# Cosformer attention and a gated feed-forward layer on one core: the q tails through GpSimd's queue, one q load moved behind the x transposes, the last product in two column pieces

## The chip, the core and the metric

The kernel runs on one core of a Trainium2 chip. A core has five engines that take their instructions in order, each from its own queue: TensorE (PE; its weight loads are shown apart as PEld), VectorE (DVE), ScalarE (ACT), GpSimd (POOL) and SyncE (SP). They wait for one another by semaphores. Sixteen DMA engines move data between HBM and the core's SBUF; DMAs are issued from the queues of SP, ACT and GpSimd. The metric is the device time of one execution in microseconds, the median of the runs.

## The reference

q, k and v are (8 batches, 8 heads, 576 positions, 64) in float32. The output is (4608, 512), one row for each batch and position.

```python
def phi(x, c, s):
    r = np.maximum(x, 0.0)
    return np.concatenate([r * c, r * s], axis=-1)
q_p, k_p = phi(q, cos_w, sin_w), phi(k, cos_w, sin_w)
kv = np.einsum('bhsf,bhsd->bhfd', k_p, v)
z = np.sum(k_p, axis=2)
num = np.einsum('bhsf,bhfd->bhsd', q_p, kv)
den = np.einsum('bhsf,bhf->bhs', q_p, z)[..., None] + 1e-06
x = (num / den).transpose(0, 2, 1, 3).reshape(B * S, H * D)

rms = np.sqrt(np.mean(x * x, axis=-1, keepdims=True) + 1e-06)
xn = x / rms * rms_g
g = xn @ w_gate
silu = g * (1.0 / (1.0 + np.exp(-g)))
out = (silu * (xn @ w_val)) @ w_out
```

w_gate and w_val are (512, 1536), w_out is (1536, 512).

## The kernel before

**Blocks.** The 4608 rows are worked through in nine blocks of 512 rows, in the order 0, 1, 2, 3, 4, 5, 6, 8, 7. Block b below 8 holds the first 512 positions of batch b. The last 64 positions of all eight batches, the tails, are 8 x 64 = 512 rows, and they are block 8. (Of batch 0 the tail is every ninth position.)

**A block** has 12 steps (`gval_step`) and an output part (`out_step`). In step n, PE forms the n-th 128 columns of the gate product and of the value product (`half_mm`, L565), four matmuls of 512 columns each, in two pairs of PSUM banks (`psG`, `psV`) by turns; ScalarE takes the silu of one (L579) and VectorE multiplies it with the other into `hT` (L580). `out_step` forms the product with w_out as seven smaller products (`prod`, L664) of sums of `hT` with sums of w_out; `side`, `q_start`, `q_end` and, in block 7, `last_part` add their results up in `osb`, and `store` writes them to HBM.

**The attention of later batches** lies in the slots of the earlier blocks. The order is written out by hand: `at(block, step, place, function, ...)` enters a call, and `run` issues it when the block gets there. Steps 12 to 17 are places in `out_step`; "post" of step 14 comes behind "post" of step 13. For batch nb from 3 on:

- Load k, v and q into `raw` (`load_kv`, `load_q`, on SP's queue) in block nb - 2, at steps 4, 6 and 8, but in block 1 (batch 3) at steps 4, 5 and 7 (lines 940 to 946).
- The feature maps of k (`k_phi`, L300 on ScalarE and L302 on VectorE) and the cast of v (`v_cast`) run from the output part of block nb - 2 into steps 0 and 1 of block nb - 1.
- In steps 0 to 3 of block nb - 1 the feature maps of q (`q_phi`, to `qp`) and their DMA transposes on SP's queue (`q_tr_dma`, L354, to `qpT`); in step 3 k times v (`kvz_pe`, L396).
- In steps 4 to 10 of block nb - 1 the four products of q with it (`nd_pe`, L458), each followed by the division (`nd_post`, L498 to L508), the sum of squares on ScalarE (`x_sq`, L524), its power -0.5 on GpSimd (L529), the norm on VectorE (`x_norm`, L536) and the DMA transpose of the rows on SP's queue (`x_tr_dma`, L549), the last of them at step 12. Block nb takes them as `xnT`; its first matmul needs all four. (For batch 2 the steps differ by one or two; the products of batch 7 are in block 8.)

**The tails of q** are loaded in four pairs of batches, each pair by two DMAs of 128 KB in rows of 256 bytes (`load_q_tails`, L147, on SP's queue), at steps (5, 9), (6, 1), (6, 2) and (6, 4). In block 6 follow their feature maps (`q_tails_phi`, steps 3, 4, 5, 7), their DMA transposes into the buffer of the k features (`q_tails_tr_dma`, L364, printed as `kp<-qp`), and at steps 5, 7, 9 and 11 the products (`nd_tails_pe`, L483).

**The ring.** k, v, q and each pair of tails take a buffer `raw` from a ring of four; a load waits until what stood in the buffer four loads earlier has been read.

**The end.** In block 7 the last products go to separate banks. `q2[1]` is a copy of the first product of the second half of the rows; products 6 and 7 are added to the copy and to the original, and `last_part` (L1015) subtracts and stores each of the four quarters of 256 columns.

Of the kernel before, what the change touches and what calls it, by code (L numbers as in the profile page):

```python
# [9 lines left out]
FP32 = mybir.dt.float32  # L10
BF16 = mybir.dt.bfloat16
AF = mybir.ActivationFunctionType
ALU = mybir.AluOpType
# [4 lines left out]
def kernel(  # L18
# [11 lines left out]
    nc = tc.nc  # L30
    B, H, S, D = q.shape
    DM = H * D
    DFF = moe_w_gate.shape[1]
    P = 128
# [3 lines left out]
    NC5 = 5  # L38
# [8 lines left out]
    V, A, G = nc.vector, nc.scalar, nc.gpsimd  # L47
# [3 lines left out]
    ring = ctx.enter_context(tc.tile_pool(name="ring", bufs=4))  # L51
# [7 lines left out]
    psG = [ps.tile([P, 512], FP32, name=f"psG{i}") for i in range(2)]  # L59
    psV = [ps.tile([P, 512], FP32, name=f"psV{i}") for i in range(2)]  # L60
    psC = [ps.tile([P, 512], FP32, name=f"psC{i}") for i in range(2)]
# [29 lines left out]
    raw = {}  # L91

    def raw_tile(which, b):
        if (which, b) not in raw:
            t = ring.tile([P, H * NC5 * D], FP32, name="raw", tag="raw")
            raw[(which, b)] = t
        return raw[(which, b)]
# [40 lines left out]
    rqt = {}  # L138

    def load_q_tails(pair):  # L140
        t = ring.tile([P, H * NC5 * D], FP32, name="raw", tag="raw")
        rqt[pair] = t[:, 0 : H * D].rearrange("p (h d) -> p h d", h=H)
        for i in range(2):
            src = q[2 * pair + i, :, 512:576, :].rearrange("h s d -> s h d")
            if 2 * pair + i == 0:
                src = q[0].rearrange("h (s c) d -> s h c d", c=NC)[:, :, NC - 1, :]
            nc.sync.dma_start(out=rqt[pair][64 * i : 64 * i + 64, :, :], in_=src)  # L147

    g4 = one.tile([4, P], FP32, name="g4")
    nc.scalar.dma_start(out=g4[:, :], in_=moe_rms_g.rearrange("(t p) -> t p", p=P))  # L150
    for c0, c1 in ((0, 4), (4, NC)):
        nc.sync.dma_start(
            out=raw_kv("k", 0)[:, :, c0 * D : c1 * D],
            in_=kv_rows(k, 0, (0, HP))[:, :, c0 * D : c1 * D],
# [58 lines left out]
    HC = DM // 2  # L213
# [22 lines left out]
    def g_spread(bank, t):  # L236
# [12 lines left out]
        out=th[:, 0:NTAB], in0=fidx[:, :], scalar1=S - 1.0, scalar2=ang,  # L249
# [341 lines left out]
    def store(blk, j, cols, src, eng=nc.sync):  # L591
        if 0 < blk < 8:
            rows = out[blk * S : blk * S + 512, :].rearrange("(p j) m -> p j m", j=4)
            eng.dma_start(out=rows[:, j, cols[0] : cols[1]], in_=src)
            return
        for i in range(2):
            b, c = (0, 2 * j + i) if blk == 0 else (2 * j + i, NC - 1)
            rows = out[b * S + 512 : b * S + S, :]
            if b == 0:
                rows = out[0:S, :].rearrange("(s c) m -> s c m", c=NC)[:, c, :]  # L600
            eng.dma_start(out=rows[:, cols[0] : cols[1]], in_=src[64 * i : 64 * i + 64])
# [49 lines left out]
    def prod(i, p, dst, first=False, cols=(0, HC)):  # L651
        c0, c1 = p * P, p * P + HC
        lhs = {
            1: (s0, 0, c0), 2: (s12, 0, c1), 3: (hT, 0, c0), 4: (hT, NM, c1),
            5: (s12, 0, c0), 6: (s3, 0, c0), 7: (s4, 0, c0),
        }[i]
        rhs = {2: (0, 0), 5: (NM, HC)}.get(i)
        for m in range(NM):
            t, o, c = lhs
            if rhs:  # L660
                w = wo[:, rhs[0] + m, rhs[1] + cols[0] : rhs[1] + cols[1]]
            else:
                w = wsum[:, {1: 0, 3: 1, 4: 2, 6: 3, 7: 4}[i], m, cols[0] : cols[1]]
            nc.tensor.matmul(  # L664
                dst, lhsT=t[:, o + m, c : c + P], rhs=w,
                start=(first and m == 0), stop=(m == NM - 1), skip_group_check=True,
            )
# [158 lines left out]
    def at(blk, n, where, f, *args):  # L826
        slots.setdefault((blk, n), {}).setdefault(where, []).append((f, args))
# [9 lines left out]
    for j in range(4):  # L837
        at(0, (8, 8, 9, 10)[j], "post", q_phi, V, 1, j, 0)
        at(0, (8, 9, 10, 10)[j], "post", q_phi, A, 1, j, 1)
        bank = (psC[0], psC[1], psV[0], psV[1])[j]  # L840
# [85 lines left out]
            at(b, m, "post", x_tr_dma, nb, j)  # L926

    for pair in range(4):
        at(*((5, 9), (6, 1), (6, 2), (6, 4))[pair], "post", load_q_tails, pair)
        n = (3, 4, 5, 7)[pair]  # L930
        at(6, n, "post", q_tails_phi, V, pair, 0)
        at(6, n, "post", q_tails_phi, A, pair, 1)
        at(6, n, "post", q_tails_tr_dma, pair)
        n = 5 + 2 * pair
        at(6, n, "pe", nd_tails_pe, pair)
        at(6, n, "pre", nd_post, 2 * pair + 1, 4)
        at(6, n, "post", x_sq, 2 * pair + 1, 4)
        at(6, n + 1, "post", x_norm, 2 * pair + 1, 4)
        at(6, n + 1, "post", x_tr_dma, 2 * pair + 1, 4)
    for nb in range(3, B):  # L940
        b = nb - 2
        for which, n in (zip("kvq", (4, 5, 7) if b == 1 else (4, 6, 8))):
            if which == "q":
                at(b, n, "post", load_q, nb)
            else:
                at(b, n, "post", load_kv, which, nb)
# [32 lines left out]
    def out_step(blk):  # L979
        bq = ((psG[0], psV[0]), (psC[0], psC[1]))  # L980
        osb = {}
        mid = slice(HC, 3 * HC)

        def begin(p):
            bank = bq[p][0]
            prod(3, p, bank[:, 0:HC], first=True)
            prod(4, p, bank[:, HC:DM])
            osb[p] = osb_tile()
            A.copy(out=osb[p][:, mid], in_=bank[:, :])
            run(blk, 12 + p, "act")  # L990

        def q_start(p):
            V.tensor_tensor(
                out=bq[p][1][:, 0:HC], in0=osb[p][:, HC : 2 * HC],
                in1=osb[p][:, 2 * HC : 3 * HC], op=ALU.add,
            )

        def side(p):
            A.copy(out=osb[p][:, mid], in_=bq[p][0][:, :])
            if blk == last_blk:  # L1000
                store(blk, p, (HC, DM), osb[p][:, HC : 2 * HC])
                store(blk, p + 2, (0, HC), osb[p][:, 2 * HC : 3 * HC])

        def q_end(p):
            V.tensor_tensor(
                out=osb_ends(p),
                in0=bq[p][1][:, :].rearrange("p (i m) -> p i m", i=2),
                in1=osb[p][:, mid].rearrange("p (i m) -> p i m", i=2), op=ALU.subtract,
            )
            store(blk, p, (0, DM), osb[p][:, 0:DM])  # L1010
            store(blk, p + 2, (0, DM), osb[p][:, DM : 2 * DM])

        def last_part(p, i, bank):
            c = 3 * HC * i
            V.tensor_tensor(  # L1015
                out=osb[p][:, c : c + HC], in0=bank[:, 0:HC],
                in1=osb[p][:, HC * (1 + i) : HC * (2 + i)], op=ALU.subtract,
            )
            store(
                blk, p + 2 * i, (HC * i, HC * i + HC), osb[p][:, c : c + HC],  # L1020
                nc.sync if p == i else nc.scalar,
            )

        def osb_ends(p):
            t = osb[p][:, 0:HC]
            ap = list(t.ap)
            return bass.AP(t.tensor, t.offset, [ap[0], [3 * HC, 2], ap[-1]])

        h_sum12(0, NM // 2)
        h_sum12(NM // 2, NM)  # L1030
        begin(0)
        run(blk, 12, "post")
        begin(1)
        q_start(0)
        h_sum0()
        run(blk, 13, "post")
        prod(5, 0, bq[0][0][:, 0:HC])
        prod(2, 0, bq[0][0][:, HC:DM])
        run(blk, 14, "act")
        side(0)  # L1040
        q_start(1)
        h_sum4()
        prod(5, 1, bq[1][0][:, 0:HC])
        prod(1, 0, bq[0][1][:, 0:HC])
        run(blk, 15, "act")
        last = blk == last_blk
        q2 = (
            (psG[1][:, 0:HC], psV[1][:, 0:HC]) if last
            else (bq[0][1][:, HC:DM], bq[1][1][:, HC:DM])
        )  # L1050
        A.copy(out=q2[0], in_=bq[0][1][:, 0:HC])
        h_sum3()
        run(blk, 14, "post")
        prod(2, 1, bq[1][0][:, HC:DM])
        if last:
            prod(7, 0, bq[0][1][:, 0:HC])
            prod(1, 1, bq[1][1][:, 0:HC])
            A.copy(out=q2[1], in_=bq[1][1][:, 0:HC])
            side(1)
            prod(6, 0, q2[0])  # L1060
            last_part(0, 0, bq[0][1])
            prod(7, 1, bq[1][1][:, 0:HC])
            last_part(0, 1, psG[1])
            prod(6, 1, q2[1])
            last_part(1, 0, bq[1][1])
            last_part(1, 1, psV[1])
            return
        prod(1, 1, bq[1][1][:, 0:HC])
        run(blk, 16, "act")
        side(1)  # L1070
        A.copy(out=q2[1], in_=bq[1][1][:, 0:HC])
        run(blk, 17, "act")
        run(blk, 12, "dve")
        prod(7, 0, bq[0][1][:, 0:HC])
        prod(6, 0, q2[0])
        q_end(0)
        prod(7, 1, bq[1][1][:, 0:HC])
        prod(6, 1, q2[1])
        q_end(1)
        run(blk, 15, "post")  # L1080
# [46 lines left out]
```

## Time and profile before

| What | us |
| --- | --- |
| median of 3 runs | 327.35 (326.6 to 328.78) |
| the profiled execution | 327.93 |
| its span in the trace | 326.2 |

| Engine | busy us | share of the span |
| --- | --- | --- |
| PE | 308.4 | 95% |
| VectorE | 234.1 | 72% |
| ScalarE | 180.3 | 55% |
| GpSimd | 41.4 | 13% |

Positions in the trace are microseconds from the span's start. The value products' first matmul groups of blocks 3, 4 and 5 begin at 122.55, 154.86 and 187.18, so a block takes 32.3 us; the one of block 6 begins at 220.75, and block 6 takes 41.1 us to that of block 8 (261.81). PE is busy for 0.9 or more of most slices of the span; the clock granted to it is full but for one stretch near 235 us and the last 1.5 us.

A line of a view of waits has the engine and line that waited, what it waited for, and us in total, times and longest. A line of the timeline has the start, the length, engine, line, operation, what is written from what, how many instructions were merged, and in brackets the idle time before and what ended it. "SPq" and "POOLq" are instructions that issue DMAs. A line of the windows has the stretch, then busy us of PE, PEld, DVE, ACT and POOL with counts, the granted clock, the DMA share and GB/s.

### The profile page before, as it was taken

How to read it: one execution, taken by the hardware profiler on the slowest of the kernel's cores; microseconds unless marked ns; L12 is line 12 of the kernel's file. 1: busy time of each engine (PE TensorE's matmuls, PEld its weight loads, DVE VectorE, ACT ScalarE, POOL GpSimd, SP SyncE). 2: the span in 40 equal slices, each digit the busy share in tenths (PEclk: the TensorE clock that was granted, in tenths of full speed). 3: DMA queues.
4: the chain of work that ended last, by engine and by line, in shares of the span. 5: the costliest groups of instructions: out<-in, count | busy, mean ns of one | idle time of the engine just before them, and what ended most of it. 6: DMA issues, size and time to landing. Idle time of an engine off the chain costs nothing.

```text
span 326.2 us, 6671 instructions
## 1 busy us (share of the span) xinstructions
PE 308.4 (95%) x2541; PEld 188.1 (58%) x2574; DVE 234.1 (72%) x459; ACT 180.3 (55%) x353; POOL 41.4 (13%) x79
## 2 busy tenths in 40 slices
PE   7899999999799999999999999989299999999995
PEld 2689564546654585458545754665145844574474
DVE  7976977989857786778678867885367747864373
ACT  5766756736764586458655865576245335433331
POOL 9670220002001100110011001100001101100000
PEclk9999999999999999999999999999789999999999
DMA  7999999789969977997779678995933130115003
GB/s 231 237 274 277 269 341 169 218 185 248 176 154 195 191 163 205 200 196 159 198 184 193 186 184 173 192 242 148 188 78 65 18 129 20 32 33 114 0 2 129
DMA packets 80383, 53.80 MB, mean 165 GB/s; under 512 B 52139, under 2 KB 74719, under 8 KB 80351
## 3 DMA queue, kind: packets, MB, share of 16 engines
q1 hardware_dynamic: 73110, 40.99, 59.6%
q0 software_dynamic: 6944, 12.13, 15.3%
q8 instruction: 20, 0.33, 0.5%
q10 hardware_dynamic: 296, 0.26, 0.2%
q14 instruction: 13, 0.10, 0.1%
HBM read 37.83 MB, written 9.44 MB: 145 GB/s over the span
## 4 chain that ended last, share of the span: by engine, by line
PE 77%; DMA 8%; DVE 5%; ACT 4%; issue 3%; SPq 1%; POOL 1%; ACTq 0%; DVEq 0%; POOLq 0%
PE psV L565 23%; PE psG L565 22%; PE psC L664 9%; PE psG L664 6%; PE psV L664 4%; DMA raw<-in_q_dram 3%; DMA hsum<-in_v_dram 2%; PE psV L716 2%; PE psG L716 2%; DVE xn L536 2%; PE psA L458 2%; DMA xnT<-xn 2%; PE psC L583 2%; PE psG L583 2%; PE psA L396 2%
## 5 line engine op out<-in xcount | busy, mean ns | idle before, releaser
L580 DVE TENSOR_TENSOR hT<-psV,sg 128x512 bf16<-128x512 f32 x99 | 68.1, 688 | 56.5 <-PE psV L565 38.0
L579 ACT ACTIVATE sg<-psG 128x512 f32<-128x512 f32 x99 | 58.6, 592 | 76.2 <-PE psG L565 74.7
L565 PE MATMUL psG<-xnT,wg 128*128 128x512 bf16 x330 | 89.1, 382 | 3.7 <-DMA xnT<-xn 1.6
L565 PE MATMUL psV<-xnT,wv 128*128 128x512 bf16 x347 | 90.7, 382 | 0.6 <-issue 0.2
L565 PEld LDWEIGHTS <-wv 128*128 128x128 bf16 x400 | 39.2, 98 | 47.4 <-issue 1.1
L565 PEld LDWEIGHTS <-wg 128*128 128x128 bf16 x400 | 36.7, 98 | 41.3 <-issue 2.9
L664 PEld LDWEIGHTS <-hsum 128*128 128x128 bf16 x480 | 46.0, 98 | 8.0 <-DVE hsum L636 2.1
L529 POOL TENSOR_TENSOR rs<-ms,mhalf 128x1 f32<-128x1 f32 x36 | 21.0, 584 | 226.4 <-ACT scr L524 226.2
L524 ACT ACTIVATE scr<-xt 128x513 bf16<-128x513 f32 x36 | 22.9, 635 | 28.4 <-DVE xt L508 27.5
L300 ACT ACTIVATE kp<-raw,tab 128x256 bf16<-128x256 f32 (+2 forms) x56 | 32.4, 617 | 2.5 <-DMA raw<-in_k_dram 2.5
L536 DVE SCALAR_TENSOR_TENSOR xn<-xt,rs,gb 128x512 bf16<-128x512 f32 (+1 forms) x37 | 26.9, 729 | 1.8 <-POOL rs L529 1.7
L300 ACT ACTIVATE qp<-raw,tab 128x512 bf16<-128x512 f32 (+1 forms) x40 | 26.0, 670 | 1.3 <-DMA raw<-in_q_dram 1.3
L508 DVE TENSOR_TENSOR xt<-psA,rec 128x512 f32<-128x512 f32 x36 | 24.9, 691 | 1.2
L664 PEld LDWEIGHTS <-hT 128*128 128x128 bf16 x192 | 18.4, 98 | 4.7 <-DVE hT L580 0.6
L664 PE MATMUL psV<-wsum,hsum 128*128 128x256 bf16 x144 | 18.7, 273 | 0.1
L302 DVE TENSOR_SCALAR kp<-raw,tab 128x256 bf16<-128x256 f32 (+1 forms) x48 | 17.8, 421 | 0.8 <-DMA raw<-in_k_dram 0.7
L664 PE MATMUL psC<-wsum,hsum 128*128 128x256 bf16 x138 | 17.7, 272 | 0.0
L302 DVE TENSOR_SCALAR qp<-raw,tab 128x512 bf16<-128x512 f32 (+1 forms) x38 | 17.2, 466 | 0.0
L458 PEld LDWEIGHTS <-qpT 128*128 128x128 bf16 x224 | 10.6, 97 | 7.0 <-issue 0.6
L630 DVE TENSOR_TENSOR hsum<-hT 128x1536 bf16<-128x1536 bf16 x16 | 14.5, 949 | 0.0
L664 PE MATMUL psC<-wo,hsum 128*128 128x256 bf16 x96 | 13.1, 273 | 0.0
L565 PE MATMUL psV<-kp,wv 128*128 128x512 bf16 x47 | 12.3, 379 | 0.1
(131 smaller groups left out, 327.0 us busy)
## 6 DMA issues: line engine op xcount, KB each, us to landing
raw<-in_q_dram SPq DMA_DIRECT2D x6, 1024.0 KB, 10.6
out_dram<-osb SPq DMA_DIRECT2D x24, 256.0 KB, 2.7
raw<-in_k_dram SPq DMA_DIRECT2D x5, 1120.0 KB, 7.8
raw<-in_v_dram SPq DMA_DIRECT2D x5, 1120.0 KB, 10.5
out_dram<-osb SPq DMA_DIRECT2D x22, 128.0 KB, 2.4
raw<-in_k_dram POOLq DMA_DIRECT2D x2, 1152.0 KB, 19.0
raw<-in_v_dram POOLq DMA_DIRECT2D x2, 1152.0 KB, 15.4
wg<-in_moe_w_gate_dram POOLq DMA_DIRECT2D x3, 512.0 KB, 14.0
```

What stands on the lines that cost most here:

```text
L300: A.activation(out=out_ap, in_=in_ap, func=AF.Relu, scale=scale)
L302: eng.tensor_scalar(out=out_ap, in0=in_ap, scalar1=scale, scalar2=0.0, op0=ALU.mult, op1=ALU.max)
L458: nc.tensor.matmul(heads[:, g, hp, :], lhsT=qpT[:, h, j * P : (j + 1) * P], rhs=kvzs[b][:, g, hp * E : (hp + 1) * E], start=True, stop=True,)
L508: V.tensor_tensor(out=xt[:, 0:DM].rearrange("p (hp g d) -> p g hp d", g=2, d=D), in0=heads[:, :, :, 0:D], in1=rec[:, :, :].unsqueeze(3).to ...
L524: A.activation(out=scr[:, :], in_=xt[:, 0 : DM + 1], func=AF.Square, scale=1.0 / math.sqrt(DM), accum_out=ms[:, :],)
L529: G.tensor_tensor(out=rs[:, :], in0=ms[:, :], in1=mhalf[:, :], op=ALU.pow)
L536: V.scalar_tensor_tensor(out=xn_of[(b, j)][:, c], in0=x_of[(b, j)][:, c], scalar=rs_of[(b, j)][:, :], in1=gb[:, c], op0=ALU.mult, op1=ALU. ...
L565: nc.tensor.matmul(bank[:, cols[0] : cols[1]], lhsT=w[:, t, n * P : (n + 1) * P], rhs=x[:, t, cols[0] : cols[1]], start=(t == 0), stop=(t ...
L579: A.activation(out=sg[:, :], in_=g[:, 0:TB], func=AF.Silu)
L580: V.tensor_tensor(out=hT[:, n, :], in0=v[:, 0:TB], in1=sg[:, :], op=ALU.mult)
L630: V.tensor_tensor(out=s12[:, m0:m1, :], in0=hT[:, m0:m1, :], in1=hT[:, NM + m0 : NM + m1, :], op=ALU.add,)
L664: nc.tensor.matmul(dst, lhsT=t[:, o + m, c : c + P], rhs=w, start=(first and m == 0), stop=(m == NM - 1), skip_group_check=True,)
```

## The change

There are three edits.

1. The four pairs of q tails go to one `raw` buffer, side by side, in place of four buffers; they are issued from GpSimd's queue, not SP's, and at steps (4, 9), (4, 11), (5, 1) and (5, 3).
2. In block 1 the load of v of batch 3 moves from step 5 to step 8 and that of q from step 7 to step 14, which stands behind the last x transpose of the block in SP's queue.
3. In block 7 the copy of the second half's first product is made in two pieces, of 160 and 96 columns, into two banks, behind `side(1)` and not ahead of it. Product 6 is made for each piece, and `last_part` subtracts and stores each. The queue of a store is given with the call.

```diff
     def load_q_tails(pair):
-        t = ring.tile([P, H * NC5 * D], FP32, name="raw", tag="raw")
-        rqt[pair] = t[:, 0 : H * D].rearrange("p (h d) -> p h d", h=H)
+        t = raw_tile("t", 0)[:, pair * H * D : (pair + 1) * H * D]
+        rqt[pair] = t.rearrange("p (h d) -> p h d", h=H)
...
-            nc.sync.dma_start(out=rqt[pair][64 * i : 64 * i + 64, :, :], in_=src)
+            nc.gpsimd.dma_start(out=rqt[pair][64 * i : 64 * i + 64, :, :], in_=src)
...
-        at(*((5, 9), (6, 1), (6, 2), (6, 4))[pair], "post", load_q_tails, pair)
+        at(*((4, 9), (4, 11), (5, 1), (5, 3))[pair], "post", load_q_tails, pair)
...
-        for which, n in (zip("kvq", (4, 5, 7) if b == 1 else (4, 6, 8))):
+        for which, n in (zip("kvq", (4, 8, 14) if b == 1 else (4, 6, 8))):
...
-        def last_part(p, i, bank):
-            c = 3 * HC * i
+        def last_part(p, i, bank, eng, c0=0, c1=HC):
+            o, t = 3 * HC * i, HC * (1 + i)
             V.tensor_tensor(
-                out=osb[p][:, c : c + HC], in0=bank[:, 0:HC],
-                in1=osb[p][:, HC * (1 + i) : HC * (2 + i)], op=ALU.subtract,
-            )
-            store(
-                blk, p + 2 * i, (HC * i, HC * i + HC), osb[p][:, c : c + HC],
-                nc.sync if p == i else nc.scalar,
-            )
+                out=osb[p][:, o + c0 : o + c1], in0=bank[:, 0 : c1 - c0],
+                in1=osb[p][:, t + c0 : t + c1], op=ALU.subtract,
+            )
+            store(blk, p + 2 * i, (HC * i + c0, HC * i + c1), osb[p][:, o + c0 : o + c1], eng)
...
-            (psG[1][:, 0:HC], psV[1][:, 0:HC]) if last
+            (psG[1][:, 0:HC], None) if last
...
-            A.copy(out=q2[1], in_=bq[1][1][:, 0:HC])
             side(1)
+            cuts = ((psV[1], 0, 160), (psC[0], 160, HC))
+            for bank, c0, c1 in cuts:
+                A.copy(out=bank[:, 0 : c1 - c0], in_=bq[1][1][:, c0:c1])
             prod(6, 0, q2[0])
-            last_part(0, 0, bq[0][1])
+            last_part(0, 0, bq[0][1], nc.sync)
             prod(7, 1, bq[1][1][:, 0:HC])
-            last_part(0, 1, psG[1])
-            prod(6, 1, q2[1])
-            last_part(1, 0, bq[1][1])
-            last_part(1, 1, psV[1])
+            last_part(0, 1, psG[1], nc.scalar)
+            for bank, c0, c1 in cuts:
+                prod(6, 1, bank[:, 0 : c1 - c0], cols=(c0, c1))
+            last_part(1, 0, bq[1][1], nc.sync)
+            last_part(1, 1, *cuts[0][:1], nc.scalar, *cuts[0][1:])
+            last_part(1, 1, *cuts[1][:1], nc.sync, *cuts[1][1:])
```

## The prediction

> **What bounds the kernel now.** I read the page first: TensorE (PE) is busy 95% of the span and its two products of the gate and value weights (L565) lead the chain of waits, so a saving has to be a stretch in which PE stands still. The query of waits, taken for the stretch from 212 to 240 us, names the largest one (columns: engine, line, what it waited for; us in total, times, longest):
>
> ```profile
> ACT sg L579 <- PE psG L565: 10.7, 5, 6.9
> PEld L483 <- DMA kp<-qp: 6.2, 1, 6.2
> PE psA L483 <- DMA kp<-qp: 5.7, 1, 5.7
> ...
> PE psG L565 <- DMA raw<-in_q_dram: 1.1, 1, 1.1
> ```
>
> PE waits 5.7 us in block 6 for the first DMA transpose of the q tails, and 1.1 us before it, where block 6 begins. The timeline of SP's queue shows what stands ahead of both (start us, us, line, operation, count):
>
> ```profile
> 207.21 4.24 SPq L549 DMA_TRANSPOSE xnT<-xn  x1
> 211.50 1.40 SPq L147 DMA_DIRECT2D raw<-in_q_dram  x2
> 212.99 2.36 SPq L549 DMA_TRANSPOSE xnT<-xn  x1
> ...
> 226.37 1.30 SPq L147 DMA_DIRECT2D raw<-in_q_dram  x2
> 227.83 1.26 SPq L354 DMA_TRANSPOSE qpT<-qp  x1
> 229.14 1.34 SPq L147 DMA_DIRECT2D raw<-in_q_dram  x2
> 230.64 1.24 SPq L354 DMA_TRANSPOSE qpT<-qp  x1
> 232.04 2.68 SPq L364 DMA_TRANSPOSE kp<-qp  x2
> ```
>
> From 226.37 on SP issues back to back, and two pairs of tail loads (L147) stand between the transposes. The chain of waits carries the landings (start, us, what), first at the end of block 1, then in blocks 5 and 6:
>
> ```profile
> 83.66 5.42 DMA xnT<-xn
> ```
> ```profile
> 212.28 6.95 DMA raw<-in_q_dram
> ...
> 232.04 3.41 DMA kp<-qp
> 235.45 0.04 issue
> ```
>
> The long wait also costs clock. In windows of 0.5 us the column before the last two is the granted clock; it falls at 232.6, 2.8 us after PE stopped (229.76), and is back at 239.4, 3.9 us after PE went on (235.50):
>
> ```profile
> 232.00:232.50 0.50, 0.00 (x0) 0.00 (x0) 0.00 (x0) 0.00 (x0) 0.00 (x0) 1.00 1.07 219
> 232.50:233.00 0.50, 0.00 (x0) 0.00 (x0) 0.00 (x0) 0.00 (x0) 0.00 (x0) 0.60 1.23 198
> ```
>
> Eight matmuls then took 1.82 + 1.65 us in place of 2 x 0.86: 1.7 us, and with the shorter matmuls about 1.9.
>
> **Block 6, the tails' wait.** Times are counted from the block's first matmul, S (219.73). PE reaches the tails' product at S + 10.0 (229.76). The eight tail loads leave SP's queue. Then the last q transpose goes out as in block 5, where it went out at 195.79 with S = 186.15: S + 9.64, as VectorE ends its half of that q feature map only at S + 9.5 (229.22). It takes 1.24 us to issue. The tails' feature maps end at S + 9.9 on VectorE (229.61), so the first tail transpose is issued at S + 10.95 and lands 3.3 us later (3.41 here with loads beside it, 3.2 the median of q transposes): S + 14.25. PE still waits 4.2 us, not 5.7. Removed: **1.5 us**, the two pairs of loads (1.30 + 1.34 us) less 1.1 that is now spent waiting for VectorE. The next thing that is late is the transpose itself. 4.2 is above the 2.8 us after which the clock fell, so I keep the clock's loss; if it stayed up, 1.9 more would go. If the loads were already in and nothing else were late, the whole 5.7 would go; the S + 9.5 of VectorE excludes that. The ends are 1.0 and 3.4.
>
> **Block 6, its start.** The first pair of tails was issued and moved ahead of the last x transpose (issued 212.99). Without it that transpose goes out at about 212.5 (block 4's 180.30 plus a block period of 32.3) and not behind 256 KB, lands before 218.6, and the 1.1 us go: **-1.1** (ends -1.2 and 0).
>
> **Blocks 4 and 5, the tails through GpSimd.** GpSimd's queue holds little, and its timeline says when it is free:
>
> ```profile
> 172.99 0.55 POOL L529 TENSOR_TENSOR rs<-ms,mhalf 128x1 f32<-128x1 f32 x1 [3.19 <-ACT scr L524]
> 176.73 0.55 POOL L529 TENSOR_TENSOR rs<-ms,mhalf 128x1 f32<-128x1 f32 x1 [3.20 <-ACT scr L524]
> 197.58 0.55 POOL L529 TENSOR_TENSOR rs<-ms,mhalf 128x1 f32<-128x1 f32 x1 [20.30 <-ACT scr L524]
> ```
>
> A DMA issue takes it 0.73 to 1.07 us (the startup's loads). Pair 0 fits between the first two powers (1.5 to 2.1 us of 3.2). The other three pairs come after 177.28 and before 197.58 in its order, and nothing makes them wait: the one buffer was last read in step 3 of block 4 (q of batch 5). So all six issues run at once, from 177.3 to 182 or 184, although two pairs are written into block 5. The powers are not delayed. In the ring of four buffers k, v and q of batch 7 now follow those of batch 6, last read by 196, and are loaded from 198 to 207: no wait.
>
> The transfers are the price. 1 MB in rows of 256 B moved at about 200 GB/s when it was alone (197 to 201 in the windows from 231 to 235): 5.2 us of all 16 engines. From 174.6 to 183.3 these are busy with k, v, q of batch 6 and the x transposes of block 5 (DMA share about 1.1 or more in windows of 1 us, but 0.39 from 178 to 179). The last x transpose was issued at 180.30 and PE needed it at 186.15; its like in block 1 landed 5.42 after its issue, so the slack is near 0.5. Below, the cost is 0, if the tails find gaps; above, it is 5.2 - 0.5 = 4.7 plus 1.9 of clock, as PE would be idle over 2.8 us. I take about half the transfer, 2.5 us, as delay: two queues share the engines, 0.9 us of pair 0 lies in front of the q load, and the gap at 178 takes some. Less the slack: **+2.0**. Nearest row: in block 5 one pair (256 KB, about 1.3 us) ahead of the same transpose, with its issues, made the 1.1 us.
>
> **Block 1, q of batch 3.** k is issued at 68.05 as before; v goes from step 5 to step 8, behind the first x transpose (74.42 to 75.6), and q behind all four. v has 7.8 us (k's landing) and lands at 83.5; ScalarE casts it from 84.54. The last x transpose was ready at 83.37 and issued at 83.66. Its 5.42 us ran while the engines moved 50 GB/s or less from 83.5 to 84.5, so they are mostly its own time, not q's: of PE's 1.57 us I take back 0.3, from the shorter issue of the one ahead. The load of q is now issued near 84.7. A q load on quiet engines (51.46, moved by about 57.7) needs some 6.5 us: it lands at 91.2. ScalarE wants it at 90.5 (90.77 - 0.3), VectorE at 91.9. ScalarE's next silu and what VectorE makes of it wait 0.7 us behind it; VectorE was idle or waiting for PE (0.25 us) before its next product, and its cast ended 0.36 us before PE used it: hidden, nearly. **-0.3** (ends -1.57, and +3.6 below).
>
> **The end.** PE's last product is cut into 160 and 96 columns: 12 matmuls for 6, the same columns, weights loading beside them, **0**. ScalarE copies its start in two pieces (0.14 us fixed from 0.36 and 0.58 for 256 and 512 columns, so 0.28 + 0.22 for 0.36) inside 0.45 us that PE spends on another product: up to +0.1. Its 512-column copy moves ahead, from 320.49 to near 318.9, so two of SP's stores leave 1.6 us earlier. The DMA engines now move six last stores in one burst from 321.9 to 324.3; with these two gone from it, the last 48 KB, issued at 322.5 as VectorE ends (322.61 before), are through by 323.6. **-0.6** (ends -1.0, +0.2).
>
> The sum: -0.3 + 2.0 - 1.1 - 1.5 - 0.6 = **-1.5**. The profiled execution took 327.93 (span 326.2 and 1.7 around it) and would take 326.4; it lies 0.6 above the median of the runs, 327.35, so I predict 325.9.
>
> **The rivals.** *The tails are hidden.* The 2.0 is 0: the transfers fill gaps and the x transpose keeps its 5.4 us. For it: the gap at 178 and the quiet stretch after 183.3; against: the issues end by 184 and the engines are full from 179 to 183. -3.5: 323.9. Chance 0.27.
>
> *The tails block the next block.* The x transposes of block 5 end behind the whole 1 MB: 4.7 us at 186.15, plus 1.9 of clock, from a wait of 2.8 us on. -3.5 + 6.6 = +3.1: 330.5. For it: small rows, all issued in 7 us; against: the two queues are separate and the load of q was there first. Chance 0.14.
>
> *q of batch 3 comes late.* A q load under load landed after 10.6 us: 95.3 here, 4.8 after ScalarE wants it, less some 0.9 of cover, so PE loses 3.9 at the first product with k and v of block 2. -1.5 + 3.9 = +2.4: 329.8. It needs stores or transposes to hold the engines from 85 to 90, where they moved little but x transposes until 87.7. Chance 0.11.
>
> *GpSimd is slow to issue.* If each of the six issues waited out one VectorE sum (0.95 us), the last would go at 186, half of the tails would come behind the x transposes, and the 2.0 would be 0.7: 324.6. Against it, the startup's issues took 0.73 to 1.07 us while VectorE was busy 0.9 to 1.0 of its time. Chance 0.05. The Trainium skill, SBUF — State Buffer, section "🔬 SBUF: two separate sides", warns of such a thing: GpSimd writes the descriptors of its DMAs itself and is locked out while VectorE runs in a two-port mode; by that rule this rival would hold, and the startup's rows do not bear it out.
>
> **How the numbers follow.** The forecast has 0.43, with 324.5 to 327.5 as its own range. Within 1% means 324.1 to 330.6, about what a measurement can tell from no change. Faster than that: most of the first rival (0.20) and the low tail of the forecast (0.07). Slower: half of the second (0.07) and a little of the third (0.03). The range of 8 in 10 runs from 323.5, leaving out a tenth below, to 329.9, leaving out most of the second rival.
>
> **What would show it.** Right: no tail load on SP; PE's wait at L483 about 4.2 us with the clock still falling; block 6 starting without a wait; a new wait of PE for an x transpose at the start of block 5, near 186; GpSimd's eight issues between 173 and 184. Wrong: a wait at L483 under 2.8 us (my order on SP and VectorE fails), block 5 starting on time or over 3 us late, ScalarE waiting over 2 us for q at 90.

## The result and the profile after

The changed kernel takes **331.91 us**, the kernel before on the same chip 327.18 us (median of 4 runs): ratio **1.0127** with an interval of 1.0084 to 1.0170. It is slower by about 4.2 us. The first execution that was profiled ran at half pace (652.62 us) and is not read. The profile below is of a repetition of the same kernel, with a median of 332.22 us beside 328.25 us, ratio 1.0111 [1.0079, 1.0143], and a profiled execution of 332.06 us.

The page (span; busy time and share by engine; granted clock in 40 slices):

```profile
span 330.2 us, 6728 instructions
PE 313.1 (95%) x2580; PEld 188.9 (57%) x2580; DVE 234.3 (71%) x460; ACT 180.3 (55%) x354; POOL 46.5 (14%) x87
PEclk9999999999999999999999969999979999999999
```

The span grew by 4.0 us (326.2 before). The clock has two dips in place of one (near 235 us before, now the second): the new one is in slice 24, from 190 to 198 us, at the start of block 5. PE's own timeline shows what is there, and a smaller stop in block 2 (start, length, engine, line, what; in brackets the idle time before and what ended it):

```profile
93.88 1.08 PE L396 MATMUL psA<-vv,kp 116*128 116x65 bf16 x30 [1.06 <-DVE vv L296]
...
191.55 1.86 PE L565 MATMUL psG<-xnT,wg 128*128 128x512 bf16 x4 [6.07 <-DMA xnT<-xn]
```

PE stops for 6.07 us in front of block 5 and then runs at a lower clock: its first group of four matmuls takes 1.86 us, 1.03 at full clock. The wait in block 6 that the change was aimed at is shorter, not gone (6.2 and 5.7 before):

```profile
PEld L483 <- DMA kp<-qp: 4.9, 1, 4.9
...
PE psA L483 <- DMA kp<-qp: 4.4, 1, 4.4
```

The chain of waits has the landings (start, us):

```profile
85.22 6.25 DMA raw<-in_q_dram
...
179.45 11.97 DMA xnT<-xn
...
237.19 3.40 DMA kp<-qp
```

The last x transpose for block 5 is issued at 179.45, earlier than before (180.30), and takes 11.97 us to land. GpSimd's timeline puts the tail loads (L147) beside it:

```profile
172.84 1.41 POOL L147 DMA_DIRECT2D raw<-in_q_dram  x2
...
176.42 4.09 POOL L147 DMA_DIRECT2D raw<-in_q_dram  x6
```

The starts of the blocks (first gate matmul) give the balance by stage, in us:

| Stretch | before | after | difference |
| --- | --- | --- | --- |
| start to block 1 | 54.54 | 54.21 | -0.33 |
| block 1 | 34.68 | 32.95 | -1.73 |
| block 2 | 32.30 | 33.53 | +1.23 |
| block 3 | 32.31 | 32.31 | 0 |
| block 4, to the start of block 5 | 32.32 | 38.55 | **+6.23** |
| block 5 | 33.58 | 34.61 | +1.03 |
| block 6 | 41.05 | 39.49 | -1.56 |
| block 8 | 31.32 | 31.06 | -0.26 |
| block 7 and the end | 34.05 | 33.49 | -0.56 |

The savings that the change was aimed at are there in small sums. One stretch outweighs them all.

### The profile page after: what moved, and what is told of

It is laid out like the page before. It is cut to its first block, busy times and chain, and to the rows that moved or that the text cites. A ratio compares the mean times of both kernels' runs of the same rounds, so it can differ in the third digit from the quotient of the medians.

```text
span 650.8 us, 6695 instructions
## 1 busy us (share of the span) xinstructions
PE 635.4 (98%) x2547; PEld 296.9 (46%) x2580; DVE 238.6 (37%) x460; ACT 182.1 (28%) x354; POOL 45.0 (7%) x87
## 3 DMA queue, kind: packets, MB, share of 16 engines
q1 hardware_dynamic: 69030, 39.99, 25.0%
## 4 chain that ended last, share of the span: by engine, by line
PE 97%; issue 1%; DMA 0%; DVE 0%; ACT 0%; ACTq 0%
PE psV L565 28%; PE psG L565 28%; PE psC L664 12%; PE psG L664 7%; PE psV L664 5%; PE psV L716 2%; PE psA L458 2%; PE psG L716 2%; PE psA L396 2%; PE psG L583 2%; PE psC L583 2%; PE psC L671 1%; PE psV L372 1%; PE psA L403 1%; DMA kp<-qp 0%
## 5 line engine op out<-in xcount | busy, mean ns | idle before, releaser
L565 PE MATMUL psV<-xnT,wv 128*128 128x512 bf16 x347 | 181.6, 679 | 2.8 <-issue 2.8
L565 PE MATMUL psG<-xnT,wg 128*128 128x512 bf16 x330 | 175.2, 677 | 4.7 <-issue 4.7
L565 PEld LDWEIGHTS <-wv 128*128 128x128 bf16 x400 | 59.2, 148 | 125.9 <-issue 125.9
L565 PEld LDWEIGHTS <-wg 128*128 128x128 bf16 x400 | 55.8, 145 | 101.0 <-issue 99.7
L664 PEld LDWEIGHTS <-hsum 128*128 128x128 bf16 x486 | 71.8, 149 | 40.8
L664 PE MATMUL psC<-wsum,hsum 128*128 128x256 bf16 (+1 forms) x144 | 36.5, 447 | 0.0
L664 PE MATMUL psV<-wsum,hsum 128*128 128x256 bf16 (+1 forms) x144 | 36.4, 448 | 0.0
L664 PE MATMUL psC<-wo,hsum 128*128 128x256 bf16 x96 | 25.8, 433 | 0.0
L565 PE MATMUL psG<-kp,wg 128*128 128x512 bf16 x46 | 24.1, 674 | 0.3 <-issue 0.3
L664 PE MATMUL psG<-wo,hsum 128*128 128x256 bf16 x96 | 24.3, 452 | 0.0
```

The costliest lines, as they stand in the source:

```text
L565: nc.tensor.matmul(bank[:, cols[0] : cols[1]], lhsT=w[:, t, n * P : (n + 1) * P], rhs=x[:, t, cols[0] : cols[1]], start=(t == 0), stop=(t ...
L664: nc.tensor.matmul(dst, lhsT=t[:, o + m, c : c + P], rhs=w, start=(first and m == 0), stop=(m == NM - 1), skip_group_check=True,)
```

## Experiments

Theory: all eight tail loads get ahead of, or in among, the last x transpose of block 5, and PE waits for it. Rivals: q of batch 3 costs the time; the end does; GpSimd's queue itself (its small rows, or its slow issue) is at fault, and not the amount of data in front of the transpose.

**The whole change again** is the profile shown above.

> The changed kernel as it is, for a profile of an ordinary execution and a closer ratio. By the theory that the tails' transfers hold the x transposes of block 5 (T1), PE waits 4 to 5 us for xnT at the start of block 5 and its clock falls there. By the theory that q of batch 3 comes late (T2), PE loses about 4 us in steps 0 to 3 of block 2, with ScalarE waiting 2 to 5 us for raw from q. By the theory that GpSimd's issues hold VectorE or its own powers (T3), the issues of the tails take well over 1 us each and VectorE's instructions beside them are longer than their like in block 3. Ratio about 1.013 by all.

Measured: 1.0111, the wait at block 5 as above, longer than the 4 to 5 us expected.

**The three edits, one by one.** The diffs are the three parts of the change, each alone on the kernel before.

> Only the first edit: tails in one buffer, by GpSimd's queue, at the earlier steps. T1 and T3: the loss is here, ratio 1.015 to 1.02 (+5 to +6 us), as the other edits take 0.3 and 0.6 us off. T2: this edit alone is faster, ratio 0.99 to 0.998 (the prediction's -0.6 to -3 us).

> Only the second edit: v of batch 3 at step 8, q at step 14. T1 and T3: ratio 0.995 to 1.001. T2: ratio 1.010 to 1.018, with the whole loss in block 2.

> Only the third edit: the last product in two column pieces. All theories: ratio 0.997 to 1.000 (the prediction's -0.6 us, ends -1.0 and +0.2). If it is over 1.003, the third edit has a part in the loss that no theory has.

| Edits | median us | ratio |
| --- | --- | --- |
| 1, tails through GpSimd | 333.5 | 1.0162 [1.0133, 1.0190] |
| 2, q of batch 3 | 327.22 | 0.9972 [0.9945, 1.0000] |
| 3, last product in pieces | 327.33 | 0.9987 [0.9961, 1.0013] |

Edit 1 alone makes the kernel slower, by 5.3 us, and has the same wait (6.06 us in front of block 5). The three differences from 1 add up to +0.0121, beside the 1.0127 of the whole: the edits don't act on each other in a way that can be measured. The end alone can't be told from no change in the times; in its profile the last stretch, from the start of block 7, takes 33.5 us (34.05 before).

**The same loads from SP's queue.** Edit 1, but issued from SP's queue, all eight ahead of the last x transpose.

```diff
-            nc.gpsimd.dma_start(out=rqt[pair]..., in_=src)
+            nc.sync.dma_start(out=rqt[pair]..., in_=src)
-        at(*((4, 9), (4, 11), (5, 1), (5, 3))[pair], "post", load_q_tails, pair)
+        at(*((4, 9), (4, 9), (4, 11), (4, 11))[pair], "post", load_q_tails, pair)
```

> The first edit alone, but on SP's queue, with all four pairs in block 4 (steps 9, 9, 11, 11), so that the same 1 MB in rows of 256 bytes is issued ahead of the last x transpose on the same queue. If it is the transfers in front of that transpose that cost (T1, whatever the queue), PE waits 4.5 to 6.5 us at the start of block 5, the clock falls, and the ratio is 1.010 to 1.018 as with GpSimd's queue. If it is something of GpSimd's queue (two queues taking turns on the engines, or GpSimd writing descriptors), the wait is under 4 us and the ratio under 1.008.

Measured: 331.35 us, 1.0106 [1.0066, 1.0146]. SP's queue (start, us, line, count):

```profile
175.49 3.68 SPq L549 DMA_TRANSPOSE xnT<-xn  x1
179.21 8.25 SPq L147 DMA_DIRECT2D raw<-in_q_dram  x8
187.56 1.38 SPq L549 DMA_TRANSPOSE xnT<-xn  x1
```

and PE's timeline:

```profile
191.55 0.59 PE L565 MATMUL psG<-xnT,wg 128*128 128x512 bf16 x1 [4.56 <-DMA xnT<-xn]
```

Here one queue carries both. The transpose stands behind the whole megabyte, is not issued before 187.56, and lands 3.86 us later (chain of waits):

```profile
187.56 3.86 DMA xnT<-xn
```

The kernel to compare with is edit 1 alone, on GpSimd's queue (PE's timeline):

```profile
192.02 1.86 PE L565 MATMUL psG<-xnT,wg 128*128 128x512 bf16 x4 [6.06 <-DMA xnT<-xn]
```

Positions in the two traces can't be set side by side, as block 4 began at 153.48 there and at 154.50 here. From there to the start of block 5 it is 38.5 us with GpSimd's queue, 37.05 with SP's and 32.3 in the kernel before. So data ahead of the transpose is enough for most of the wait without GpSimd's queue; the other 1.5 us come with that queue.

The 3.86 us are not the transpose's time with nothing in front of it: between its issue and 189.75 the engines still moved 0.39 MB, of which the transpose itself has 0.13. In the two versions below that spread the loads out on SP's queue, an x transpose of block 1 landed in 3.5 and 3.4 us. I take 3.86 us as the most that it needs.

**The same bytes in long rows.** Edit 1, with GpSimd's loads in rows of 2 KB in place of 256 bytes, taken from other positions of q. The tails hold other values of q here.

```diff
-            src = q[2 * pair + i, :, 512:576, :].rearrange("h s d -> s h d")
+            src = q[2 * pair + i, 0, 0:512, :].rearrange("(s r) d -> s (r d)", r=8)
```

> The first edit alone, with the same number of bytes a load, but taken from other positions of q in rows of 2 KB and not 256 bytes (so the tails hold other values of q). If the number of small rows sets the cost, the 1 MB passes in some 3 us, PE's wait at the start of block 5 falls from 6.1 to 2 to 3.5 us and the ratio to 1.000 to 1.008. If the bytes do, or their being on a second queue at all, the wait stays over 5 us and the ratio at 1.013 to 1.018.

Measured: 331.62 us, 1.0143 [1.0092, 1.0194]. The transpose (chain of waits) still takes 10.31 us, where 3.86 were enough behind the loads on SP's queue, and PE waits 4.44 us. That is between the two expectations, under 3.5 if the rows set the cost and over 5 if they don't:

```profile
180.40 10.31 DMA xnT<-xn
```

The queues between 172 and 192 us (packets, MB, share of the 16 engines' time) show what became of the rows. First the changed kernel, then the one with long rows, then the one with the loads on SP:

```profile
q1 hardware_dynamic: 3891, 3.12, 88.7%
q0 software_dynamic: 384, 1.05, 26.7%
```
```profile
q0 software_dynamic: 384, 1.05, 21.7%
```
```profile
q1 hardware_dynamic: 8400, 4.27, 120.5%
```

GpSimd's megabyte (q0) goes out in 384 packets of about 2.7 KB with either row length. On SP's queue the same data raises the count from 3891 to 8400 (with 0.1 MB of other traffic shifted into the stretch); over the whole span SP's queue had 73110 packets before and 69030 after, 4080 fewer for 1 MB, so about 256 bytes each. Small rows were my explanation for a slow transfer; in GpSimd's queue they are bundled, and its megabyte costs 26.7% of 20 us, 5.3 us of all engines, 4.3 us in long rows. That is close to the 5.2 us in the prediction. With long rows the wait was 1.6 us shorter, but the intervals of the two ratios of edit 1 overlap. So the small rows are at most about a quarter of the wait, and the runs do not resolve whether they are that.

**One pair only.** The whole change, but with only the first pair by GpSimd at (4, 9); the others on SP in block 5.

```diff
-            nc.gpsimd.dma_start(out=rqt[pair]..., in_=src)
+            (nc.sync if pair else nc.gpsimd).dma_start(out=rqt[pair]..., in_=src)
-        at(*((4, 9), (4, 11), (5, 1), (5, 3))[pair], "post", load_q_tails, pair)
+        at(*((4, 9), (5, 1), (5, 2), (5, 3))[pair], "post", load_q_tails, pair)
```

> All three edits, with only pair 0 by GpSimd in block 4 and the other pairs on SP's queue at steps 1, 2 and 3 of block 5: a quarter of the bytes ahead of the x transposes. In the changed kernel the last of them landed 8.1 us later than the 3.86 us that it took behind all loads on SP; a quarter of that is 2.0, and PE has 2.0 us of slack there. T1: PE waits 0 to 1 us at the start of block 5, ratio 0.987 to 0.995. If any load by GpSimd in that stretch costs, whatever its size, the wait is over 2 us and the ratio over 0.998.

Measured: 326.33 us, 0.9968 [0.9947, 0.9990]. Block 5 starts at 184.83 without a wait: this pair, 256 KB issued at 172.37, costs nothing there. But the six loads in block 5 push SP's later issues back (the load of q of batch 7 leaves 22.4 us after block 5 begins, 21.1 with four loads there in the version after the next), and the wait turns up one block on, in front of block 6. So the ratio is above the 0.987 to 0.995 that the theory gave (PE's timeline):

```profile
219.34 1.02 PE L565 MATMUL psG<-xnT,wg 128*128 128x512 bf16 x3 [2.03 <-DMA xnT<-xn]
```

**All four pairs by GpSimd, held back.** The whole change, with all loads at (5, 0) behind a one-element product on GpSimd that needs VectorE's feature map of q of batch 6, so that they start only within block 5.

```diff
+    def hold_gp():
+        G.tensor_tensor(out=hold[:, :], in0=qp_of((6, 0))[:, 0, 0:1],
+                        in1=qp_of((6, 0))[:, 0, 0:1], op=ALU.mult)
+    at(5, 0, "post", hold_gp)
-        at(*((4, 9), (4, 11), (5, 1), (5, 3))[pair], "post", load_q_tails, pair)
+        at(5, 0, "post", load_q_tails, pair)
```

> All three edits, still by GpSimd's queue, but GpSimd is held until VectorE's first feature map of block 5 (a product of one element, S + 3.5), so that the 1 MB moves in the stretch where only the q transposes run. If the loss is the transfers ahead of block 5's x transposes (T1), that wait is gone: ratio 0.988 to 0.996. If GpSimd's packets (384 for the 1 MB, some 2.7 KB each) hold back the small packets of a transpose whenever they run together, the first q transposes of block 5 land later than their 3.2 us and PE waits 1 to 4 us at its product with q in steps 4 to 6, ratio 0.996 to 1.005.

Measured: 329.55 us, 1.0049 [1.0026, 1.0072]. Block 5 starts in time (184.81). The ratio is not the 0.988 to 0.996 that the theory alone gave, as the damage moved into the block. A q transpose that needs 3.2 us (the median before) now takes (chain of waits):

```profile
191.66 9.83 DMA qpT<-qp
```

PE waits for it and, with SP's queue now late (the first x transpose leaves 17.3 us after block 5 begins, 15.1 in the next version), again at block 6:

```profile
PE psG L565 <- DMA xnT<-xn: 2.5, 1, 2.5
...
PE psA L458 <- DMA qpT<-qp: 1.0, 1, 1.0
```

Between the two PE loses another 1.6 us, for a copy of ScalarE's (L1080), which had itself waited 1.5 us for the load of v.

**The loads spread out on SP's queue.** All three edits, but the tails on SP: two pairs into a buffer of their own in blocks 3 and 4, two into the ring in block 5.

```diff
-        t = raw_tile("t", 0)[:, pair * H * D : (pair + 1) * H * D]
+        if pair < 2 and "t" not in raw:
+            raw["t"] = one.tile([P, 2 * H * D], FP32, name="qtails")
+        t = raw["t"] if pair < 2 else raw_tile("t", 0)
+        t = t[:, pair % 2 * H * D : (pair % 2 + 1) * H * D]
-            nc.gpsimd.dma_start(out=rqt[pair]..., in_=src)
+            nc.sync.dma_start(out=rqt[pair]..., in_=src)
-        at(*((4, 9), (4, 11), (5, 1), (5, 3))[pair], "post", load_q_tails, pair)
+        at(*((3, 1), (4, 1), (5, 1), (5, 2))[pair], "post", load_q_tails, pair)
```

> All three edits, but the tails on SP's queue where the DMA engines have little to do: pairs 0 and 1 into a buffer of their own at step 1 of blocks 3 and 4, pairs 2 and 3 into the ring at steps 1 and 2 of block 5. T1: no wait for xnT at the start of blocks 5 and 6; at the tails' product PE still waits 4.2 to 4.5 us and the clock falls, as VectorE's feature map comes at S + 9.5. Ratio 0.986 to 0.992 (the prediction's first rival, -3.5 us). If moving the loads early is itself what costs, the ratio stays over 1.0.

Measured: **324.45 us**, 0.9902 [0.9867, 0.9937]. SP's queue in block 5 has the loads between the q transposes:

```profile
189.22 2.97 SPq L357 DMA_TRANSPOSE qpT<-qp  x2
192.25 1.30 SPq L150 DMA_DIRECT2D raw<-in_q_dram  x2
193.71 1.25 SPq L357 DMA_TRANSPOSE qpT<-qp  x1
195.00 1.28 SPq L150 DMA_DIRECT2D raw<-in_q_dram  x2
196.44 2.19 SPq L357 DMA_TRANSPOSE qpT<-qp  x1
```

PE has no wait for a DMA in block 5 nor in front of block 6 (217.91). What the change was meant to bring is 3.2 us, once the loads cost nothing; the wait in block 6 is as long as in the changed kernel (`L486` is the line of L483 here):

```profile
PE psA L486 <- DMA kp<-qp: 4.5, 1, 4.5
```

So the tail loads are not what is late there.

**The tails' feature maps earlier too.** The kernel just shown, with the tails' feature maps in steps 0 to 3 of block 6, their transposes in steps 3 and 5, and the feature maps and transposes of q of batch 7 behind them.

```diff
-            n = j + (nb == 2)
+            n = j + (nb == 2) if nb < 7 else (4, 5, 6, 8)[j]
-        n = (3, 4, 5, 7)[pair]
-        at(6, n, "post", q_tails_phi, V, pair, 0)
-        at(6, n, "post", q_tails_phi, A, pair, 1)
-        at(6, n, "post", q_tails_tr_dma, pair)
+        at(6, pair, "post", q_tails_phi, V, pair, 0)
+        at(6, pair, "post", q_tails_phi, A, pair, 1)
+        at(6, (3, 3, 3, 5)[pair], "post", q_tails_tr_dma, pair)
```

> As the run with the tails loaded in quiet stretches, and in block 6 the tails' feature maps change places with those of q of batch 7 (tails at steps 0 to 3, batch 7, whose products come in block 8 only, at 4, 5, 6, 8); the tails' transposes are issued in step 3, behind the product that reads their buffer. If the wait at the tails' product is set by VectorE's feature map and SP's order, as the prediction has it, it falls from 4.4 us to under 1 and the clock stays up: ratio 0.965 to 0.975. If the DMA transpose itself or the buffer sets it, it stays near 4 us and the ratio at 0.986 to 0.992.

Measured: **317.39 us, 0.9686 [0.9656, 0.9717]**: 10.3 us less than the kernel before, and the fastest version here. The page, and SP's queue in block 6:

```profile
span 315.5 us, 6681 instructions
...
PEclk9999999999999999999999999999999999999999
```
```profile
223.84 4.08 SPq L367 DMA_TRANSPOSE kp<-qp  x3
228.60 3.44 SPq L357 DMA_TRANSPOSE qpT<-qp  x2
```

The tails' first transpose leaves 6.5 us after block 6 begins (217.31), not 11 (237.19 - 226.16), PE does not wait for it, and the clock never falls. Block 6 takes 33.6 us (40.6 in the kernel just shown). The edit moves the feature maps and SP's order together, so their shares are not told apart.

**q of batch 3 ahead of the transpose again.** The fastest version, with that one load moved back from step 14 to 12.

```diff
-        for which, n in (zip("kvq", (4, 8, 14) if b == 1 else (4, 6, 8))):
+        for which, n in (zip("kvq", (4, 8, 12) if b == 1 else (4, 6, 8))):
```

> The fastest run so far (tails in quiet stretches, their feature maps ahead of batch 7's) with the load of q of batch 3 at step 12 of block 1 and not 14, ahead of the last x transpose on SP's queue and not behind it. PE's wait of 0.8 us in block 2 for the cast behind that q should go; the last x transpose of the block comes behind 1 MB and may wait 3 us more than its 3.9. If it still lands before PE needs it, ratio 0.964 to 0.968; if not, PE waits 1 to 2 us at the start of block 2 and the ratio is 0.970 to 0.975.

Measured: 319.67 us, 0.9757 [0.9729, 0.9784]; the interval lies clear of that of the version with step 14. PE waits again where block 2 begins:

```profile
88.94 1.02 PE L568 MATMUL psG<-xnT,wg 128*128 128x512 bf16 x3 [1.98 <-issue]
```

The profile names no transfer as the end of this wait; that it is the load's place follows from the edit, which changes nothing else. The stop also costs clock. The granted clock falls at about 90.0, 3.0 us after PE stopped (86.96) and 1.0 after it went on, and the first four groups of the block take 5.1 us where 3.5 is full clock. The wait of 0.8 us for the cast behind that q is gone, as expected.

## Why the prediction was wrong

The prediction was 325.9, range 323.5 to 329.9; the time is above the range. The mechanism was in it as a rival, "The tails block the next block", with 330.5 and a chance of 0.14.

- **Block 6, the tails' wait (-1.5):** right. PE waits 4.4 us for a predicted 4.2; block 6 is 1.56 us shorter; the clock still falls. That what is late next is VectorE's feature map and the order on SP, taken together, is shown from both sides: loads that cost nothing leave the wait at 4.5, earlier feature maps and transposes take it away.
- **Block 6, its start (-1.1):** right; there is no wait there.
- **Block 1 (-0.3):** near in sum (-1.73 + 1.23 = -0.5) by luck, wrong inside. I read 5.42 us as the transpose's own time and gave back 0.3 of PE's 1.57; all of it went. The load of q was in its way, as the version with step 12 shows. q landed at 91.47 for a predicted 91.2; ScalarE waited 2.67 us for it, not 0.7, as it was free earlier, and PE 1.06 at L396.
- **The end (-0.6):** the trace has -0.56; the edit alone is not resolved from no change.
- **Blocks 4 and 5, the tails through GpSimd (+2.0):** this step failed. It cost 6.07 us of waiting and 2.3 of clock (the first three groups of matmuls, 191.55 to 196.44, take 4.9 us for 2.6): **8.4** in place of 2.0.

Within that step, the order of GpSimd's work was as forecast: two issues between the powers, six at 176.42, with 0.68 us each, although VectorE was busy 0.67 or more of each microsecond from 176 to 181. So the loads were not slow to be issued, and the rival with VectorE is out. (The row that the prediction held against it was weaker than it says: beside the startup's issues VectorE was busy 0.47 to 1.00 of each microsecond from 2 to 8 us, not 0.9 to 1.0.) The rule of the Trainium skill that stood beside this rival (SBUF — State Buffer, section "🔬 SBUF: two separate sides") is not borne out here; whether VectorE was in the mode that the page speaks of, the trace does not say.

Two numbers of the step were wrong, in opposite directions. The slack was not 0.5 us. Issued at 179.45, a transpose of at most 3.86 us lands by 183.3, and PE wanted it at 185.48: at least 2.2 us. The trace before showed this: there the transpose was issued at 180.30, and the engines had almost nothing to move from 183 to 184 (DMA share 0.12) and nothing at all from 184 to 186 (0.00). The 5.42 us of block 1 had the load of q in them. The delay was not 2.5 us, "about half the transfer", but at least 11.97 - 3.86 = 8.1, more than the upper end of 5.2. The halving was the mistake: "two queues share the engines" was taken as a reason that the transpose would get through early, when it was issued behind six of the eight loads (at 179.45; the last load was out by 180.5). It landed 38.4 us after block 4 began, later than in the kernel where the whole megabyte stood ahead of it on its own queue (36.9).

One pair alone (256 KB) cost no wait at block 5 and four pairs cost 6.07, which fits; but that pair also leaves earlier than the other three (172 against 176 to 180), so amount and place are not told apart. That PE's idle time would also cost clock was seen, and its 1.9 us is in the rival; with the delay sized as "all of it" the forecast would have been that rival's.

Still open is why the delay is 8.1 us or more when the megabyte needs 5.3 us of all engines. In the last stretch of the wait the engines are shown full and move little (0.5 us windows: the last three columns are clock, DMA share, GB/s):

```profile
189.00:189.50 0.50, 0.00 (x0) 0.00 (x0) 0.00 (x0) 0.00 (x0) 0.00 (x0) 0.91 1.16 24
189.50:190.00 0.50, 0.00 (x0) 0.00 (x0) 0.00 (x0) 0.00 (x0) 0.00 (x0) 0.50 2.12 131
```

The Trainium skill, DMA: Bandwidth & Descriptors, sections "🔬 Queues, rings and completion order" and "🔬 SWDGE vs HWDGE vs iDMA", has each DMA engine take turns between the queues, one whole packet at a time, with packets of preferably at most 4096 bytes. Packets of 2.7 KB by turns with those of a transpose would fit the stretched transposes of this case (11.97 us, and 9.83 with the loads held back); the runs show the counts and the landings, not the turns.

## What to carry to other kernels

A load moved to another queue was not out of the way here: a transpose issued behind it on SP's queue came 8 us late. So look in the trace for where the DMA engines are quiet, and charge at least the whole transfer to the last transfer that someone waits for, not a share of it. Take a transfer's own time from an instance with nothing in front of it before working out slack. When a wait has several causes in a row, find the second one before moving the first: here the loads were worth 1.3 us of the wait (5.7 to 4.4), and the order of the feature maps and transposes behind them about 7 us of time (the two versions with loads on SP, 324.45 and 317.39).

## What the hardware showed unexpectedly

- GpSimd's queue moved rows of 256 bytes in 384 packets of 2.7 KB per megabyte, SP's in about 4096 of 256 bytes.
- The transposes beside GpSimd's packets were stretched: the x transpose from 3.86 us to 11.97, a q transpose from 3.2 to 9.83. Loads on SP between q transposes (512 KB) caused no wait in that block; the amounts differ, so how much of it is the queue is not settled.
- Eight tail loads on SP's queue took 8.25 us to issue in a row behind other transfers, where two took 1.30 on a quieter queue, 1.03 us each in place of 0.65. What held the issues up the profile does not say.
- There is no one length of stop after which the clock falls. It fell 2.8 us after PE stopped in block 6 of the kernel before, 3.9 in front of block 5 after the change and 4.4 in its block 6, and 2.2 with the held loads, where PE waited 2.5 us and, 1.5 us before that, another 1.6. In the last version above a stop of 1.98 us was enough, with the fall 1.0 us after PE had gone on; with one pair only, a stop of 2.03 us cost no clock at all. So the 2.8 us that the prediction goes by is one instance and no threshold. The clock was back 3.9 us after PE went on in the kernel before, and about 4.7 and 3.4 after the two stops of the changed one. The Trainium skill, TensorE: Matmul & The Clock Gate, section "🔬 Part 1: The HAM clock gate (the "warmup" mystery)", has it fall after an idle window of about 3.4 us that runs freely; 2.8 and 1.98 are shorter than that, and 2.2 too, if the stop before it does not count.
